# Where the weight sums of the next expert are made: an attention and mixture-of-experts kernel with an order written out by a planner

## The chip, the cores and the metric

The kernel runs on one core of one Trainium2 chip. The metric is the device time of one execution in microseconds (us). Three executions of the kernel before took 963.54, 964.22 and 965.71 us; their median is 964.22 us. The profile shows one further execution, which took 963.27 us.

Engine names are those of the profile: PE is the matrix engine (TensorE), PEld its weight loads, DVE VectorE, ACT ScalarE, POOL GpSimd, SP the engine that only issues DMAs here.

## The reference

```
def phi(x): return np.where(x > 0, x, np.exp(x) - 1.0) + 1.0
# q, k, v: [8 batches, 8 heads, 576 tokens, 64], fp32
q_p, k_p = phi(q), phi(k)
kv  = einsum('bhsd,bhse->bhde', k_p, v);  z = sum(k_p, axis=2)
att = einsum('bhsd,bhde->bhse', q_p, kv) / (einsum('bhsd,bhd->bhs', q_p, z) + 1e-6)
x   = att.transpose(0, 2, 1, 3).reshape(4608, 512)
P = exp(x @ w_gate - max)                     # [4608, 8], w_gate: [512, 8]
for _ in range(8):                            # Sinkhorn: rows, then columns
    P /= P.sum(1) + 1e-9;  P /= P.sum(0) + 1e-9;  P *= 4608 / 8
for e in range(8):                            # w1: [8, 512, 1024], w2: [8, 1024, 512]
    out += P[:, e:e+1] * (maximum(x @ w1[e], 0) @ w2[e])
```

The experts hold nearly all the arithmetic: eight times a 4608 x 512 x 1024 and a 4608 x 1024 x 512 product.

## The kernel before, in words

**Stages.** The attention works on 16 jobs n = 0 to 15 (a batch and half of its heads each). Each loads k, q and v (line 274, from SP's queue except n = 2 to 5, which POOL issues) and leaves its part of the transposed x in SBUF (`xT`, fp16). Expert 0 runs beside it, nine groups g of 512 tokens, as plain matmuls (lines 590 and 859) for the first five groups and in the seven-product form below for layer 1 of the last four. The Sinkhorn loop runs on DVE in the same stretch. Experts 1 to 7 follow, from about 200 us on.

**Seven products in place of eight.** From expert 1 on both layers use a Strassen-Winograd scheme: each matrix is cut into 2 x 2 blocks, and seven block products replace eight, at the price of sums of blocks. The sums of x (four per group) are made once, with the raw blocks written to a scratch tensor in DRAM (`xd`) and read back for every expert (line 665). The sums of w1 are `W` (four DVE additions, line 922, tiles W1, W2, W4, W3 in this order) and of w2 `T` (four DVE subtractions, line 938, T1 to T4, kept in a tile that the profile calls `h`). They are made anew for each expert, from weights that have landed. The sums of the hidden layer are `S` (line 968, four per group). The seven products of layer 1 are m1 to m7 (lines 737 and 742), the adding of a PSUM bank and a kept partial with the relu is line 780 on DVE; the job of that kind which closes product 7 is recorded as "22" (`pe_id[(u, "b22")]`). Layer 2's seven products are line 997. DVE adds most of their banks into the accumulator `acc`, times P (line 1011); the second product's bank goes by ACT (line 1018) and is added by POOL, from SBUF to SBUF (line 1021).

**Units.** A unit is one group of one expert, so nine units (0 to 8) make an expert. In the hand-written order (`order`, line 1085) a unit's own layer-1 products are called a1 to a7 and b1 to b7 (its two pairs of column blocks), A1 to A6 are those of the next unit, and y1 to y7 are layer 2 of the unit two before. PE runs exactly this order:

`y1 y5 y2 a7 y6 y3 a4 b1 b5 y7 b6 b3 b2 b7 A1 A5 y4 b4 A6 A3 A2`

Product y7 adds into the bank that y6 has used, and waits until DVE has taken that bank out.

**The planner.** Everything else is ordered by a list scheduler in the kernel (`_Plan`), which runs when the program is built. Each job names its engines, the jobs it depends on, the buffers it takes and a priority (lower goes first); the scheduler plays the program through with costs of its own and so fixes, for each engine, the order of its instructions. On the chip each engine runs its list strictly in order, and the framework adds semaphore waits for the data and the buffers alone. A dependency that is not one of data, like the gates below, acts on the place in the list and makes no wait on the chip. A table at the end (`ranks`, line 1098) overrides priority, and sometimes the engine, of single jobs by number; it covers the attention, expert 0 and two jobs of expert 1. Jobs 838 to 1045 are those of the last four groups of expert 0.

**Places that the change touches.** The weight loads (line 219, issued from POOL's queue, which also holds POOL's additions) come from expert 2 on in four parts per matrix, into two buffers in turn, so that expert e takes the buffer of e-2; each part is gated by a product 5 of the preceding expert. `W` and `T` have six slots each for four tiles per expert: the first two sums find a free slot early, the third and fourth need the slots of the preceding expert's first and second. The sums carry priority -900 for experts from 2 on, ahead of all else on DVE. In `x_blocks`, `f_st` (line 644) stores the sums of x and `f_raw` (lines 613 and 615, three DMAs per group) the raw blocks, both from SP's queue; `in_prev[0]` is the last q, k or v load that was issued, which is that of job 15 when `x_blocks` runs.

Of the kernel before, what the change touches and what calls it, by code (L numbers as in the profile page):

```python
# [122 lines left out]
def kernel(  # L123
# [20 lines left out]
    NG = N // 512  # L144
# [7 lines left out]
    add = S_.add  # L152
# [87 lines left out]
    w_last, in_prev, w_part = [None], [None], {}  # L240
# [318 lines left out]
    t_close = add(("none", 0.0), f_close, deps=front_ids, prio=0.0)  # L559
# [45 lines left out]
    def x_blocks(g):  # L605
        bs = range(512 * g // S, (512 * g + 511) // S + 1)
        deps = [xt_done[(b, c)] for b in bs for c in range(NDT)]
        t0 = 512 * g
        early = g < NX
        gt_ = S_.grp(p_xse if early else p_xst)  # L610

        def f_raw(_):
            nc.sync.dma_start(out=xd[g // 2][:, g % 2, 0], in_=xT[:, 0:2, t0:t0 + 256])
            for b in range(2):
                nc.sync.dma_start(out=xd[g // 2][:, g % 2, 1 + b], in_=xT[:, 2:4, t0 + 256 * b:t0 + 256 * b + 256])
        last = first = None
        for i in range(3):
            def f_T(_, i=i):
                if i == 0 and early:
                    h_ = (len(p_xse["order"]) - 1) % 2  # L620
                    gt_["tile"] = (acc[NA - 1][:, 2 * h_:2 * h_ + 2, :].bitcast(FP16)
                                   .rearrange("p a (b c t) -> p (a b) c t", b=2, c=2))
                elif i == 0:
                    gt_["tile"] = accp[2].tile([P, 4, 2, 256], FP16, tag="xst", name="xst")
                T = gt_["tile"]
                lo, hi = xT[:, :, t0:t0 + 256], xT[:, :, t0 + 256:t0 + 512]
                if i == 0:
                    nc.vector.tensor_tensor(out=T[:, 0], in0=hi[:, 0:2], in1=lo[:, 0:2], op=ALU.subtract)
                    nc.vector.tensor_tensor(out=T[:, 2], in0=hi[:, 2:4], in1=hi[:, 0:2], op=ALU.subtract)
                elif i == 1:  # L630
                    nc.vector.tensor_tensor(out=T[:, 1], in0=hi[:, 2:4], in1=T[:, 0], op=ALU.subtract)
                else:
                    nc.vector.tensor_tensor(out=T[:, 3], in0=lo[:, 2:4], in1=T[:, 1], op=ALU.subtract)
            last = add(("dve", 0.8 if i == 0 else 0.42), f_T,
                       deps=deps + [v_land[NG + 1 + g] if early else t_close, last] +
                       ([xst_of[g - 1][2]] if i == 0 and g > NG - NL else []),
                       acq=[gt_] if i == 0 else [], use=[gt_], prio=g - 8.0)
            first = first or last
            x_users.append(last)

        xst_of[g] = gt_, last, first

        def f_st(_):
            nc.sync.dma_start(out=xd[g // 2][:, g % 2, 3:7].rearrange("p i c t -> p (i c t)"),
                              in_=gt_["tile"].rearrange("p i c t -> p (i c t)"))
        ti = add(("sp", 0.45), f_st, deps=[last], use=[gt_], prio=0.0)
        out_ = [add(("dma", 1.5), lambda _: None, deps=[ti], use=[gt_], prio=0.0, lat=2.6)]
        ti = add(("sp", 0.9), f_raw, deps=deps + [ti], prio=0.0)
        out_.append(add(("dma", 1.0), lambda _: None, deps=[ti], prio=0.0, lat=2.6))
        x_users.extend(out_)  # L650
        if early:
            xse_done.append(out_[0])
        return out_
# [250 lines left out]
    def combos(e):  # L904
        gw1, tw1, gw2, tw2 = w_t[e]
        gW, tW, gT, tT = {}, {}, {}, {}
        last = wt_prev[0]
        for n, i in enumerate((1, 2, 3, 4) if e == 0 else (1, 2, 4, 3)):
            gW[i] = S_.grp(p_W)

            def f_W(_, i=i):
# [8 lines left out]
                else:  # L920
                    a0, a1, op = w[:, 2:4, 0:512], gW[2]["tile"], ALU.subtract
                nc.vector.tensor_tensor(out=gW[i]["tile"], in0=a0, in1=a1, op=op)
            last = tW[i] = add(("dve", 0.685), f_W, deps=tw1 + [t_close, last, pe_id.get((NG * (e - 1) + min(n, 1) + 5, "b22"))],
                               acq=[gW[i]], use=[gw1] + ([gW[i // 2]] if i in (2, 4) else []),
                               prio=-900.0 if e > 1 else 4.5)
        wt_prev[0], last = last, wt_prev[1]
        for i in range(1, 5) if e > 0 else ():
            gT[i] = S_.grp(p_T)

            def f_T(_, i=i):  # L930
# [5 lines left out]
                          (w[:, 4:8, 256:512], w[:, 0:4, 256:512]),  # L936
                          (w[:, 4:8, 0:256], gT[2]["tile"])][i - 1]
                nc.vector.tensor_tensor(out=gT[i]["tile"], in0=a0, in1=a1, op=ALU.subtract)
            last = tT[i] = add(("dve", 0.685), f_T, deps=tw2 + (h0_users if e == 1 else []) + [x_closed[0], last, pe_id.get((NG * (e - 1) + (i + 15) // 2, ("a22", "b22")[(i + 15) % 2]))],
                               acq=[gT[i]], use=[gw2] + ([gT[i // 2]] if i in (2, 4) else []),  # L940
                               prio=-900.0 if e > 1 else 5.0)
        wt_prev[1] = last
# [130 lines left out]
    x_closed[0] = add(("none", 0.0), f_xclose, deps=x_users, prio=0.0)  # L1073
    for e in range(1, E):
        if e >= 2:
            wg = [[pe_id[(NG * (e - 1) + u + v, f"{n}5")] for v in (0, 2) for n in "ab"] for u in (0, 4)]
            w_t[e] = (load_w1(e, prio=float(e), parts=4, gates=wg[0], deps=w_t[e - 1][1][1:]) +
                      load_w2(e, prio=float(e), parts=4, gates=wg[1], deps=w_t[e - 1][3][1:]))
        co = combos(e)
        for g in range(NG):  # L1080
            if e == E - 1 and g == NG - 1:
                unit_plain(e, g, *co[0:2])
            else:
                unit(e, g, *co)
# [10 lines left out]
    for d, k_ in zip(chain, chain[1:]):  # L1095
# [85 lines left out]
        809:-98.0027 810:-49.9991 811:-50.0237 812:-50.0231 813:-50.0006 814:-50.0132 815:-50.0009 816:-50.0093  # L1181
        817:-49.9718 818:-49.9847 819:-50.0192 820:-49.9832 821:-49.976 822:-49.9994 823:-50.0009 824:8.7515
        825:-98.0234 826:-50.0075 827:-50.0078 828:8.7506 829:8.7428 830:8.7509 831:8.7491:act 832:-49.9745:act
        833:8.7572 834:8.7455 835:-50.0054 836:-49.9853:act 837:-50.0162:dve 838:-49.9829 839:-49.9826 840:-98.0237
        841:-50.0114 842:-50.0075 843:-98.0243 844:-49.9841 845:-50.0201 847:-49.9742 850:-98.0255 851:-49.976
        852:-50.0132 853:-50.024 854:-49.9976 855:8.7518 856:-50.021 857:-50.0078 858:-49.9745 859:-49.9844
        860:-50.0225 861:-98.0156 862:-50.0198 863:-49.9997 864:-50.0087 865:-50 866:-49.976 867:-98.0231 868:-50.0027
        869:8.7542 870:-50.0057 871:8.7443 872:-98.0222 873:-50.0216 874:-50.0177 875:-98.0015 876:-50.0159
        877:-50.0201 878:-50.021 879:8.7443 880:8.4603 881:-50.006 882:8.4591 883:-50.0195 884:8.4594 885:-98.0243
        886:-50.0258 887:-50.0174:act 888:-98.0216 889:-50.0009:act 890:-49.9991 891:-49.9991:dve 892:-98.0036:act  # L1190
        893:-50.018 894:-49.9829 895:-49.982 896:-97.9988 897:8.7434 899:8.744 902:-98.0225 903:-50.018 904:-50.0186
        905:8.7431 906:8.4666 907:-98.0249 908:-50.0237 909:-98.0231 910:-49.9823 911:-98.0231 912:-50.0177
        913:-49.9739 914:8.4609 915:-50.0069 916:8.4672 917:-49.9754 918:8.4672 919:-98.0264 920:-50.0249 921:-49.9988
        922:-50.0231 923:8.7347 924:-50.0186 925:-98.0234 926:-49.9733 927:-50.0234 928:-50.0018 929:-97.9991
        930:8.7368 931:-50.0063 932:-50.0036 933:15.4873 934:8.4711 935:15.4924 936:8.4543 937:-50.0186
        938:-97.9892:dve 939:-50:act 940:-50.0069:dve 941:-50.0237 942:8.7497:act 943:-50.0225:act 944:-49.9907
        945:-49.9997:dve 946:-50.0231 947:-98.0039 948:-50.0009 949:-50.0021 951:-50.0069 954:-49.9739 955:-50.0159
        956:-50.0066 957:8.7422 958:-49.9727 959:-97.9997 960:8.4681 961:8.7521 962:-50.0153 963:-98.0252 964:-50.003
        965:-49.9895 966:8.4729 967:-50.0267 968:8.472 969:8.7506 970:-50.003 971:-50.0018 972:8.4726 973:-98.0261
        974:8.4741 975:-50.0027 976:8.7362 977:-50.021 978:-50.0156 979:-50.0222 980:-50.0021 981:-50.0204 982:15.5131  # L1200
        983:-50.0114 984:-50.0021 985:15.5068 986:8.7497 987:15.5047 988:-50.0255 989:15.4978 990:-50.0009
        991:8.7575:act 992:-50.0222 993:-50.0234 994:-49.9895:dve 995:8.7395:act 996:-50.0162:act 997:-49.9757
        998:-50.0081 999:8.7452 1000:8.7473 1001:-50.024 1003:-50.0069 1006:15.4879 1007:-50.0015 1008:15.4912
        1009:-50.0129 1010:-50.0015 1011:-50.0102 1012:-49.979 1013:-98.0243 1014:-50.015 1015:-50.0252 1016:15.4912
        1017:-50.0018 1018:-50.0039 1019:-50.0159 1020:-50.0063 1021:-50.0186 1022:-50.0003 1023:-50.0234 1024:15.4918
        1025:8.7578 1026:15.4846 1027:-50.0003 1028:-98.0255 1029:-50.0234 1030:-50.0135 1031:-50.0171 1032:-49.988
        1033:-50.015 1034:15.5164 1035:15.5173 1036:15.5077 1037:15.5077 1038:8.756 1039:15.5089 1040:-50.0198
        1041:15.5035 1042:-50.0105:act 1043:-50.0105:dve 1044:-50.0246:act 1045:-98.0045:act 1129:-390.9916
        1144:-390.9907
    """  # L1210
    for w in ranks.split():
        n, p, *en = w.split(":")
# [35 lines left out]
```

## Time and profile before

| what | value |
|---|---|
| median of three executions | 964.22 us (963.54 to 965.71) |
| the profiled execution | 963.27 us |
| its span, first to last instruction | 961.4 us |
| PE busy | 952.0 us, 99% of the span |
| DVE, ACT, POOL busy | 771.1, 570.1, 153.1 us |
| granted PE clock | 0.999 of full speed |
| DMA, mean over the span | 127 GB/s |

The difference between the execution's time and its span, 1.9 us, lies ahead of the first and behind the last instruction. PE's busy time is the union of the modelled stretches of its matmuls. A matmul's duration there includes its passage through the array (273 ns for 256 columns), while in a run of them one starts every 109 ns; an idle gap shorter than the difference does not show as idle. The time from one start to the next is therefore what tells whether PE lost time.

### The profile page before, as it was taken

Reading aid. Unit: us, or ns where it says so; the run is one execution under the profiler, and the core shown is the slowest. Engines: PE = TensorE matmul, PEld = TensorE weight load, DVE = VectorE, ACT = ScalarE, POOL = GpSimd, SP = SyncE. Lnnn points to the kernel's source line nnn. Section 1 sums busy time; section 2 is a strip of 40 time slices with the busy share of each in tenths; the row PEclk is TensorE's granted clock in tenths of the full one; section 3 lists DMA queues with packets and bytes.
Section 4 is the critical chain, followed back from the end, with each engine's and each line's share of the span. In section 5 each row is a group of like instructions: output and inputs, shape, how many; then the busy total and the mean of one; then the engine's idle time right before and its main releaser. Section 6 shows DMA issues by size and latency. Waiting matters only on the chain.

```text
span 961.4 us, 18780 instructions
## 1 busy us (share of the span) xinstructions
PE 952.0 (99%) x7265; PEld 650.3 (68%) x7265; DVE 771.1 (80%) x1530; ACT 570.1 (59%) x1031; POOL 153.1 (16%) x199
## 2 busy tenths in 40 slices
PE   9999999999999999999999999999999999999998
PEld 4666666566676667766676666766677666766676
DVE  6898888977887777987877778977778778877776
ACT  6897755865555555555555555555555555555552
POOL 4100000001111111121112111121112111111111
PEclk9999999999999999999999999999999999999999
DMA  9987982234344432444334432533324433425545
GB/s 318 340 318 262 270 238 82 33 89 100 77 137 108 99 81 65 106 99 100 77 98 96 99 93 67 143 96 94 78 69 100 99 99 78 137 78 150 156 106 132
DMA packets 109946, 121.83 MB, mean 127 GB/s; under 512 B 7840, under 2 KB 92960, under 8 KB 109856
## 3 DMA queue, kind: packets, MB, share of 16 engines
q1 hardware_dynamic: 84320, 96.23, 31.9%
q0 software_dynamic: 25136, 23.87, 14.8%
q8 instruction: 57, 0.93, 0.4%
q10 hardware_dynamic: 400, 0.52, 0.2%
q14 instruction: 33, 0.27, 0.1%
HBM read 119.69 MB, written 17.69 MB: 143 GB/s over the span
## 4 chain that ended last, share of the span: by engine, by line
PE 89%; DVE 5%; DMA 2%; ACT 2%; issue 1%; POOL 0%; DVEq 0%
PE ye L997 32%; PE hq L737 20%; PE att L737 10%; PE ye L859 6%; PE Zye L997 5%; PE Zye L737 5%; PE hq L742 3%; PE hq L590 2%; PE att L742 1%; DVE S L968 1%; DMA kqin<-in_k_dram 1%; DMA kqin<-in_q_dram 1%; DVE acc L1011 1%; DVE h L780 1%; PE xt_ps L418 1%
## 5 line engine op out<-in xcount | busy, mean ns | idle before, releaser
L1011 DVE SCALAR_TENSOR_TENSOR acc<-ye,P_sb,acc 128x256 f32<-128x256 f32 x620 | 266.4, 476 | 106.0 <-PE ye L997 104.2
L997 PEld LDWEIGHTS <-S 128*128 128x128 f16 x1984 | 194.0, 98 | 49.4 <-issue 3.8
L1021 POOL TENSOR_TENSOR acc<-acc,h 128x256 f32<-128x256 f32 x124 | 102.7, 844 | 602.4 <-ACT h L1018 602.4
L997 PE MATMUL ye<-h,S 128*128 128x256 f16 x1488 | 192.8, 273 | 2.6 <-DVE acc L1011 2.6
L997 PEld LDWEIGHTS <-h 128*128 128x128 f16 x1488 | 145.6, 98 | 39.9
L777 ACT ACTIVATE h<-hq 128x512 f16<-128x512 f32 x134 | 80.1, 598 | 142.4 <-PE hq L737 123.4
L737 PEld LDWEIGHTS <-W 128*128 128x128 f16 x896 | 87.6, 98 | 81.4
L737 PE MATMUL hq<-xs,W 128*128 128x512 f16 x448 | 133.3, 379 | 0.0
L737 PE MATMUL att<-xs,W 128*128 128x512 f16 x448 | 133.3, 379 | 0.0
L737 PE MATMUL hq<-xs,w 128*128 128x512 f16 x448 | 124.1, 379 | 0.0
L780 DVE CUSTOM_DVE_ANT_0 h<-att,s 128x512 f16<-128x512 f32 x126 | 86.3, 685 | 26.4 <-ACT s L764 26.4
L737 PEld LDWEIGHTS <-w 128*128 128x128 f16 x672 | 65.7, 98 | 54.8
L774 ACT ACTIVATE h<-Zye 128x512 f16<-128x512 f32 x134 | 80.1, 598 | 33.9 <-PE Zye L737 27.0
L1018 ACT ACTIVATE h<-Zye,P_sb 128x256 f32<-128x256 f32 x124 | 52.1, 471 | 78.4 <-PE Zye L997 78.4
L764 ACT COPY s<-hq 128x512 f32<-128x512 f32 x126 | 73.5, 583 | 38.3 <-PE hq L737 30.7
L780 DVE CUSTOM_DVE_ANT_0 h<-hq,s 128x512 f16<-128x512 f32 x126 | 86.3, 685 | 9.0 <-PE hq L737 9.0
L757 ACT COPY Zye<-hq 128x512 f32<-128x512 f32 x134 | 77.9, 582 | 24.4 <-PE hq L737 17.3
L968 DVE TENSOR_TENSOR S<-h 128x1024 f16<-128x1024 f16 x124 | 85.0, 686 | 5.9 <-ACT h L777 5.9
L771 ACT COPY s<-att 128x512 f32<-128x512 f32 x126 | 74.6, 592 | 0.0
L859 PE MATMUL ye<-w,h 128*128 128x512 f16 x296 | 73.5, 379 | 0.0
L737 PE MATMUL Zye<-xs,w 128*128 128x512 f16 x224 | 66.6, 379 | 0.0
L997 PE MATMUL ye<-w,S 128*128 128x256 f16 x496 | 64.3, 273 | 0.0
(119 smaller groups left out, 1100.3 us busy)
## 6 DMA issues: line engine op xcount, KB each, us to landing
xs<-xd SPq DMA_DIRECT2D x196, 256.0 KB, 4.1
w<-in_moe_w_dram POOLq DMA_DIRECT2D x48, 256.0 KB, 4.1
out_dram<-acc SPq DMA_DIRECT2D x67, 128.0 KB, 2.4
kqin<-in_k_dram SPq DMA_DIRECT2D x12, 576.0 KB, 5.0
kqin<-in_q_dram SPq DMA_DIRECT2D x12, 576.0 KB, 6.6
vin<-in_v_dram SPq DMA_DIRECT2D x12, 576.0 KB, 7.2
xs<-xd SPq DMA_DIRECT2D x49, 128.0 KB, 2.7
xd<-xT SPq DMA_DIRECT2D x27, 128.0 KB, 5.2
```

Source lines behind the costliest of these rows:

```text
L737: nc.tensor.matmul(dst, lhsT=lhs(0, c), rhs=X(b)(c), start=(first and c == 0), stop=(c == 1), skip_group_check=True)
L757: nc.scalar.copy(out=Zt[1], in_=gX["tile"])
L764: nc.scalar.copy(out=gs2["tile"], in_=gX["tile"])
L771: nc.scalar.copy(out=gs5["tile"], in_=gR["tile"])
L774: nc.scalar.activation(out=hd(0, 0), in_=Zt[1], func=AF.Relu)
L777: nc.scalar.activation(out=hd(1, 0), in_=gX["tile"], func=AF.Relu)
L780: nc.vector._custom_dve(TENSOR_ADD_SAT, out=dst, in0=ps, in1=sb, s0=3.0e38, s1=0.0)
L859: nc.tensor.matmul(gy[tt]["tile"], lhsT=hx(f, P * tt, P), rhs=gw2["tile"][:, f, :], start=(f == 0), stop=(f == NFT - 1))
L968: nc.vector.tensor_tensor(out=gS[i]["tile"], in0=a0, in1=a1, op=op)
L997: nc.tensor.matmul(bank(g_)[:, s, :], lhsT=lhs(s, kk), rhs=rhs(kk), start=(new and s == 0 and kk == 0), stop=(kk == 3), skip_group_check=True)
L1011: nc.vector.scalar_tensor_tensor(out=dst(), in0=bank(g_)[:, s, :], scalar=P_sb[:, gg, e:e + 1], in1=dst(), op0=ALU.mult, op1=ALU.add)
L1021: nc.gpsimd.tensor_tensor(out=dst(), in0=dst(), in1=gst["tile"], op=ALU.add)
```

## The change

Three edits of dependencies, one of gates, and new entries in `ranks`:

- `f_W`: the first sum of w1 for expert e may be placed from unit 3 of the preceding expert on (before: unit 5), the others from unit 4 on (before: unit 6).
- `f_T`: sums 1 to 4 of w2 may be placed after the closing job "b22" of units 5, 6, 7 and 8 of the preceding expert. Before they were placed after a22 and b22 of unit 8 and a22 and b22 of unit 0 of the expert itself.
- The gates of the parts of w1 were products 5 of pairs 0a, 0b, 2a and 2b, those of w2 4a, 4b, 6a and 6b; now they are 0a, 0b, 1a, 2a and 2b, 3a, 4a, 4b.
- `f_raw` may only be placed behind the last q, k or v load.
- 56 entries of `ranks` get other values: 44 for PE jobs of the last four groups of expert 0, ten for DVE and ACT jobs there (of which three also get or lose a fixed engine), and two for DVE jobs of unit 0 of expert 1.

No instruction is added or removed.

```diff
@@ x_blocks
-        ti = add(("sp", 0.9), f_raw, deps=deps + [ti], prio=0.0)
+        ti = add(("sp", 0.9), f_raw, deps=deps + [ti, in_prev[0]], prio=0.0)
@@ combos
-            last = tW[i] = add(("dve", 0.685), f_W, deps=tw1 + [t_close, last, pe_id.get((NG * (e - 1) + min(n, 1) + 5, "b22"))],
+            last = tW[i] = add(("dve", 0.685), f_W, deps=tw1 + [t_close, last, pe_id.get((NG * (e - 1) + min(n, 1) + 3, "b22"))],
...
-            last = tT[i] = add(("dve", 0.685), f_T, deps=tw2 + (h0_users if e == 1 else []) + [x_closed[0], last, pe_id.get((NG * (e - 1) + (i + 15) // 2, ("a22", "b22")[(i + 15) % 2]))],
+            last = tT[i] = add(("dve", 0.685), f_T, deps=tw2 + (h0_users if e == 1 else []) + [x_closed[0], last, pe_id.get((NG * (e - 1) + i + 4, "b22"))],
@@ the loop over experts
-            wg = [[pe_id[(NG * (e - 1) + u + v, f"{n}5")] for v in (0, 2) for n in "ab"] for u in (0, 4)]
+            wg = [[pe_id[(NG * (e - 1) + int(x[0]), x[1] + "5")] for x in w.split()] for w in ("0a 0b 1a 2a", "2b 3a 4a 4b")]
@@ ranks (job:priority[:engine]); a few of the 56
-        879:8.7443 880:8.4603 882:8.4591 884:8.4594 906:8.4666 916:8.4672
+        879:-50.0126 880:-50.0249 882:-50.0183 884:-97.9976 906:-50.0063 916:-98.0036
-        933:15.4873 934:8.4711 935:15.4924 982:15.5131 985:15.5068 1034:15.5164 1035:15.5173 1041:15.5035
+        933:-98.0231 934:11.585 935:11.5853 982:11.585 985:11.5886 1034:11.5973 1035:-49.9841 1041:-49.9778
-        938:-97.9892:dve 943:-50.0225:act 997:-49.9757 1045:-98.0045:act 1129:-390.9916 1144:-390.9907
+        938:-50.027 943:-390.9841:act 997:-390.9853:act 1045:8.7398 1129:-390.0186 1144:-390.0144
```

## The prediction

> **What bounds the kernel now.** I read the page's busy times first, then the list of waits, then the chain around one place that the waits named, then the timelines of PE, DVE and POOL there, and last the sums by unit. The page and the waits:
>
> ```profile
> PE 952.0 (99%) x7265; PEld 650.3 (68%) x7265; DVE 771.1 (80%) x1530; ACT 570.1 (59%) x1031; POOL 153.1 (16%) x199
> ...
> PE ye L997 <- DVE acc L1011: 2.6, 6, 0.4
> ```
>
> PE is the bound, so a gain can only come out of time in which PE starts nothing. The second line is the only repeated wait of PE: layer 2 waited six times for an eviction on DVE. The six lie 110.07 us apart (280.25, 390.31, 500.38, ...), one at each change of expert from 1 to 2 up to 6 to 7. The chain and the timelines of PE and POOL at the first:
>
> ```profile
> 277.70 0.50 issue
> 278.20 1.21 DVE h L938
> 279.41 0.80 DVE acc L1011 x2
> 280.20 0.04 issue
> 280.25 1.03 PE ye L997 x8
> ...
> 279.22 0.60 PE L742 MATMUL att<-xs,W 128*128 128x256 f16 x4
> 280.25 1.03 PE L997 MATMUL ye<-h,S 128*128 128x256 f16 x8 [0.43 <-DVE acc L1011]
> ...
> 277.00 1.86 POOL L1021 TENSOR_TENSOR acc<-acc,h 128x256 f32<-128x256 f32 x2 [10.76 <-ACT h L1018]
> ```
>
> The columns are start, duration and what. T1, the first sum of the next expert's w2, stands on DVE ahead of the two evictions of y6, and y7 can't start before they are out. Four products begin at 279.22 at 0.109 us each (eight take 0.87), so y7 was due at 279.66 and came at 280.25: 0.59 us are lost, of which 0.43 shows as idle. T1 also runs long:
>
> ```profile
> L938 DVE TENSOR_TENSOR h<-w x14: 679/692/1216, 197.9 to 850.8; 128x1024 f16<-128x1024 f16 x14
> L922 DVE TENSOR_TENSOR W<-w x16: 637/678/682, 129.4 to 832.2; 128x1024 f16<-128x1024 f16 x16
> ```
>
> Minimum, median and maximum in ns: the same kind of sum takes 692 in the median and 1216 at these six places, where it begins 0.52 us into POOL's second addition (277.68 to 278.86). The units of expert 2, from unit 3 to 6, 8 and the one behind it:
>
> ```profile
> 322.96:335.12 12.16, 12.16 (x87) 8.21 (x85) 7.54 (x16) 6.94 (x13) 2.10 (x3) 1.00 0.50 130
> 335.12:347.28 12.16, 12.16 (x87) 8.23 (x85) 11.01 (x23) 6.94 (x13) 2.54 (x3) 1.00 0.30 67
> 347.28:359.44 12.16, 12.16 (x86) 8.23 (x85) 8.13 (x17) 6.94 (x13) 2.10 (x3) 1.00 0.47 121
> 359.44:371.59 12.15, 12.15 (x86) 8.20 (x85) 11.52 (x24) 6.94 (x13) 2.54 (x3) 1.00 0.19 32
> ...
> 383.74:396.05 12.31, 11.88 (x102) 9.75 (x100) 12.28 (x24) 6.61 (x13) 2.34 (x3) 1.00 0.43 128
> 396.05:408.20 12.15, 12.15 (x86) 8.20 (x85) 10.43 (x21) 6.93 (x14) 2.44 (x4) 1.00 0.50 92
> ```
>
> Behind the length come the busy times of PE, PEld, DVE, ACT and POOL. PE is full everywhere but in the boundary unit, where DVE's 12.28 us exceed a unit's 12.15.
>
> **The change, part by part.**
>
> *T1 and T2 leave the boundary.* T1 holds DVE from 278.20 to the next start at 279.33, 1.13 us; T2 (284.68 to 285.28) 0.60. Without T1 the evictions of y6, done by PE at about 277.6, follow the sum S at 278.20 and end 0.87 us later, at 279.07 (their x2 rows take 0.87). That is 0.59 ahead of y7's due time of 279.66, so the whole 0.59 goes, not a part. What is late next: W4 and W3 stay, since their slots are those of W1 and W2 of the old expert, read last by b5 (279.22 to 279.66) and b6 (behind y7). W4 then runs from about 279.85 to 280.5, y7's own evictions follow at 280.6, and y4 that needs them comes seven products later. DVE in this unit falls to 12.28 - 1.13 - 0.60 = 10.55 us, below the 11.52 that a unit without loss carries. T3 and T4 keep their places (300.44, 302.61), because they wait for the slots that y5 and y6 of the old expert's unit 8 read. Six boundaries give 6 x 0.59 = 3.5 us. Ends: 2.6 (the idle that shows) and 3.6.
>
> *The four sums in the middle.* T1 and T2 take the places behind b22 of units 5 and 6 that W1 and W2 hold now, with the same 0.68 us, so these two units stay at 8.13 and 11.52. W1 and W2 go to units 3 and 4, of the same parity in the two-unit pattern: 7.54 + 0.68 = 8.2 and 11.01 + 0.60 = 11.6 of 12.16. The cover is DVE's idle time there: behind W1's present place DVE idles 0.45 us before its next eviction (356.62 to 357.30, next 357.75), and in unit 4 0.42 (345.59). Cost 0. If the cover were gone, each sum would cost up to the 0.59 of the row above; below nothing it can't be, since PE is full in these units.
>
> The places matter because of POOL. POOL adds at 350.58 to 351.99 and from 362.74, so the sum at 356.62 is alone, and units 3 and 4 repeat this 24.3 us earlier. At the boundary the sum S at 277.58 remains, 0.1 us ahead of POOL's second addition; one S, at 669.2, began behind it, took 957 ns against a median of 681, and PE lost nothing there.
>
> The Trainium skill has the rule for this in "SBUF — State Buffer", section "Who interferes with whom": a DVE instruction with two SBUF inputs and a GpSimd instruction that reads SBUF exclude each other, and the one that starts first blocks the other for its whole length. The trace agrees with 1216 ns against 692 where POOL began first. The rule speaks against the change in one respect: with S blocked in full at each boundary, T1's 0.52 us of blocking would be S's, the evictions would end near 279.6, and the 3.5 would hold with under 0.1 us to spare; by the rows, with S ahead of POOL, it holds with 0.59.
>
> *The weight parts.* Eight issues per expert of 0.74 to 0.78 us on POOL stay eight. Gates make no wait on the chip, only a place in POOL's list, so today's issues at 285.50, 291.16, 303.84, 315.91, 327.63, 340.23, 351.94 and 364.54 should become, by my estimate from the places of the new gates among POOL's additions, 285.5, 291.2, 291.9, 303.8, 315.9, 316.7, 327.6 and 340.2. The first waits 6.65 us for the old buffer as it does now. None stands long before a POOL addition: the next after 291.9 is at 301.95. w2's buffer is read last by y3 of the old unit 8 at 302.4 to 303.3, before 315.9. A part lands in about 4.1 us: w1 is whole near 308, first needed near 332; w2 near 344.4, needed at 356.6. What shares the DMA engines are the x blocks on SP's queue. The tightest is the fifth block of each pair of units: one issued at 304.3 lands at 308.6 and is used at 310.2, 1.6 us later, with a part issued at 303.84 beside it. That overlap stays for two of the pairs and goes for the third (351.94). Cost 0; ends: 0, and one x block late by the 1.3 us that an overlapped landing took more (5.4 against 4.1, at 285.2), which its 1.6 of slack still holds.
>
> *Raw copies behind the last load.* SP's list today:
>
> ```profile
> 75.77 0.34 SPq L644 DMA_DIRECT2D xd<-acc  x1
> 76.15 0.44 SPq L613 DMA_DIRECT2D xd<-xT  x1
> 76.63 1.37 SPq L615 DMA_DIRECT2D xd<-xT  x2
> 78.10 0.43 SPq L644 DMA_DIRECT2D xd<-acc  x1
> 78.58 0.45 SPq L613 DMA_DIRECT2D xd<-xT  x1
> 79.07 1.61 SPq L615 DMA_DIRECT2D xd<-xT  x2
> 80.78 0.44 SPq L274 DMA_DIRECT2D kqin<-in_k_dram  x1
> ```
>
> The stores of the sums (L644) stay, since they keep their dependencies; the nine copies of groups 0 to 2 go behind the load at 99.73. The loads of job 12 then issue some 3.5 us sooner (77.3), job 14's v 2.4 sooner, job 15's k at least 0.8. The copies then take 5.5 us of SP at about 100.2 to 105.7; behind them stands the store at 103.29, which nothing needs before 128.48. PE has expert 0's work throughout, so earlier data shortens only PE's in-order waits: from 104 to 115 us I find 0.48, 0.23, 0.13 and 0.22 us between starts in excess of the products' own steps, 1.1 in all. I take half, -0.5, because the first of them hangs on job 15's k. Ends: -1.1 and +0.5 (one more wait of the largest size).
>
> *New ranks.* They reorder 44 PE jobs of expert 0 between about 130 and 200 us, where PE is full (69.66 of 70 us) and DVE has 59.66. The same products run, so only waits can change. Between starts I find 0.24 + 0.43 + 0.19 + 0.13 = 1.0 us lost there. Ends: -1.0, and +1.5, three waits of the 0.5 size. I take 0, as neither sign shows in any row.
>
> The sum: -3.5 - 0.5 = -4.0 us against the profiled execution, 963.27 to 959.3. The median stands 0.95 above that execution, which gives 960.2.
>
> **The rivals.** *The boundary stall stays under another name* (W4, W3 or an eviction takes T1's place, or T1 is not moved because its parts land late). For it: DVE still has 24 - 2 jobs there. Against it: 1.6 us of room by the sum above, and 12 us between landing and use. It gives 964.22 - 0.5 = 963.7.
>
> *The sums in the middle push evictions.* For it: units 4 and 6 leave DVE only 0.5 us. Against it: unit 6 holds W2 today and PE lost nothing. If W1 and W2 each cost 0.59 in six experts, 7.1 us come back: 964.2 - 4.0 + 7.1 = 967.3. With this one, the result is slower than before once each of the 24 moved sums costs over 0.25 us.
>
> *Expert 0's new order makes PE wait.* ACT is busy 10.0 of 10 us from 180 to 190 and DVE 9.69 from 170 to 180, so products put earlier can find their banks not yet evicted. At a wait of 0.5 us for one in five of the 44 jobs this costs 4.4 us: 964.6, no change. It takes 5.9 to be slower by more than can be told from no change.
>
> **How the numbers follow.** 0.2% of 964.22 is 1.93 us, about what a measurement of this kernel tells from none: faster means below 962.29. Forecast 0.74 (the ends above, all at once, are 958.5 and 963.6; as a faster result its own range is 958.5 to 962.2); stall under another name 0.09 (963.7, same); middle sums 0.06 (967.3, slower); expert 0's order 0.11, of which 0.03 slower, 0.06 same and 0.02 still faster. So faster 0.76, same 0.15, slower 0.09. The range for 8 in 10 cuts the forecast's far end by little and reaches over the same-size cases: 958.8 to 964.2.
>
> **What would show it.** Right: no wait of PE for DVE in line 997 any more, no L938 row above 0.7 us after 200 us, T1 and T2 where W1 and W2 stand now, 109.5 us from expert to expert in place of 110.07. SP shows L613 and L615 only behind the last L274. Wrong: a PE wait at the old place with W or an eviction ahead; L997 or L737 waiting in units 3 to 6; PE idle over 1 us more between 100 and 200 us; a load in POOL's list that blocks its additions.

## The result, and the profile after

The changed kernel takes 959.84 us (median of six executions, 958.73 to 960.26), the kernel before 964.51 us (six, 963.54 to 965.71). The ratio is 0.9949 with a 95% interval of 0.9937 to 0.9962: 4.7 us faster, and clear of what a measurement tells from no change. The profiled execution took 960.04 us, with a span of 958.3 us against 961.4.

The page's busy times and the longest entries of the waits of PE after the change:

```profile
span 958.3 us, 18782 instructions
...
PE 950.7 (99%) x7265; PEld 650.3 (68%) x7265; DVE 768.7 (80%) x1529; ACT 571.7 (60%) x1032; POOL 153.4 (16%) x199
...
PE yw L510 <- DVE warm L498: 1.3, 1, 1.3
PE num_ps L402 <- DVE xn L407: 1.2, 1, 1.2
PE xt_ps L418 <- ACT P_sb L441: 0.3, 1, 0.3
```

No wait of line 997 for DVE is left. The first remaining one belongs to the warm-up products at the start; the second is new and comes back below. The same boundary as before, in the timelines of PE, DVE and POOL:

```profile
277.03 1.04 PE L997 MATMUL ye<-h,S 128*128 128x256 f16 x8
277.90 1.04 PE L997 MATMUL ye<-w,S 128*128 128x256 f16 x8
278.77 1.04 PE L742 MATMUL hq<-xs,w 128*128 128x256 f16 x8
279.65 0.60 PE L742 MATMUL att<-xs,W 128*128 128x256 f16 x4
280.08 1.04 PE L997 MATMUL ye<-h,S 128*128 128x256 f16 x8
...
278.11 0.68 DVE L968 TENSOR_TENSOR S<-h 128x1024 f16<-128x1024 f16 x1
278.71 1.65 DVE L1011 SCALAR_TENSOR_TENSOR acc<-ye,P_sb,acc 128x256 f32<-128x256 f32 x4
...
277.43 1.95 POOL L1021 TENSOR_TENSOR acc<-acc,h 128x256 f32<-128x256 f32 x2 [10.77 <-ACT h L1018]
```

The evictions of y6 (the first two of the four on DVE at 278.71) now follow the sum S at once and are out by about 279.58, half a microsecond before y7's turn at 280.08. PE goes from product to product without a gap: 279.65 plus four steps of 0.109 is 280.09. The sums of the weights no longer run long (minimum, median and maximum in ns), and the units have no hole. The second fence has the boundary unit of the kernel before (unit 8 of expert 2), and the third units 3 to 6, 8 and the next of the changed kernel. Each row of the two goes from one y1 to the next:

```profile
L938 DVE TENSOR_TENSOR h<-w x14: 679/683/693, 198.4 to 847.7; 128x1024 f16<-128x1024 f16 x14
```

```profile
383.61:396.40 12.79, 12.37 (x105) 9.98 (x103) 12.76 (x25) 6.94 (x13) 2.64 (x3) 1.00 0.43 129
```

```profile
322.64:334.80 12.16, 12.16 (x85) 8.22 (x84) 8.12 (x16) 6.94 (x13) 2.10 (x3) 1.00 0.47 125
334.80:346.96 12.16, 12.16 (x86) 8.22 (x85) 11.53 (x23) 6.94 (x13) 2.55 (x3) 1.00 0.30 73
346.96:359.11 12.15, 12.15 (x85) 8.22 (x84) 8.11 (x16) 6.94 (x13) 1.41 (x2) 1.00 0.31 99
359.11:371.27 12.16, 12.16 (x85) 8.22 (x84) 11.53 (x23) 6.94 (x13) 1.87 (x2) 1.00 0.03 10
...
383.45:395.65 12.20, 12.20 (x104) 9.97 (x102) 12.11 (x24) 6.94 (x13) 2.65 (x3) 1.00 0.44 139
395.65:407.81 12.16, 12.16 (x85) 8.23 (x84) 9.17 (x18) 6.94 (x13) 2.89 (x4) 1.00 0.65 105
```

PE is busy all of every unit, the one at the boundary (383.45) too, which takes 12.20 us where it took 12.79. DVE is still nearly full there, 12.11 of 12.20 us, and PE loses nothing by it.

To say where PE lost time I take, over all its products, the time from one start to the next less the step that products of that shape show when nothing holds them (216 ns for 512 columns, 109 ns for 256, and so on). By this the profile of before lost 3.5 us at the six boundaries, and that of after nothing. But the spans differ by 3.1 only, since the changed kernel's profile lost more between 60 and 120 us: 2.99 against 2.36 us. In that stretch of many short products I count only excesses over 0.1 us, against each shape's median step; with other steps the totals move by 1 us and more, but the difference stays between 0.3 and 0.7. (The expectations below count with slightly other steps, which gives some 0.2 us less.) That part differs between profiles of the same program, as the experiments show, and the profiled execution of the kernel before was one of its faster ones (963.27 against a median of 964.5).

### The profile page after: what moved, and what is told of

It is laid out like the page before. It is cut to its first block, busy times and chain, and to the rows that moved or that the text cites. A ratio compares the mean times of both kernels' runs of the same rounds, so it can differ in the third digit from the quotient of the medians.

```text
span 958.3 us, 18782 instructions
## 1 busy us (share of the span) xinstructions
PE 950.7 (99%) x7265; PEld 650.3 (68%) x7265; DVE 768.7 (80%) x1529; ACT 571.7 (60%) x1032; POOL 153.4 (16%) x199
## 4 chain that ended last, share of the span: by engine, by line
PE 95%; DMA 2%; ACT 1%; DVE 1%; issue 0%; POOL 0%; SPq 0%; DVEq 0%; ACTq 0%
PE ye L997 34%; PE hq L737 20%; PE att L737 10%; PE ye L859 7%; PE Zye L997 6%; PE Zye L737 5%; PE hq L742 4%; PE hq L590 2%; DMA kqin<-in_k_dram 2%; PE att L742 2%; PE Zye L742 1%; PE xt_ps L418 1%; PE kv_ps L335 1%; PE num_ps L402 1%; PE qt_ps L363 1%; ACT e L290 1%
## 5 line engine op out<-in xcount | busy, mean ns | idle before, releaser
L997 PE MATMUL Zye<-w,h 128*128 128x256 f16 x496 | 64.3, 273 | 0.0
```

What stands on the lines that cost most here:

```text
L997: nc.tensor.matmul(bank(g_)[:, s, :], lhsT=lhs(s, kk), rhs=rhs(kk), start=(new and s == 0 and kk == 0), stop=(kk == 3), skip_group_check=True)
```

## The experiments

Every comparison is with the kernel before on the same chip.

### The sums and the weight parts alone

```diff
-  ... min(n, 1) + 5, "b22" ...        (f_W)
+  ... min(n, 1) + 3, "b22" ...
-  ... (i + 15) // 2, ("a22", "b22")[(i + 15) % 2] ...   (f_T)
+  ... i + 4, "b22" ...
-  gates 0a 0b 2a 2b | 4a 4b 6a 6b
+  gates 0a 0b 1a 2a | 2b 3a 4a 4b
```

> Only the three edits of the sums and weight parts; raw copies and ranks as before. My theory (the gain is the boundary stall): 3.5 us faster than before, near 961.0; the six waits of PE line 997 for DVE are gone, the time from expert to expert goes from 110.07 to 109.5 us, the stalls of 104 to 115 us stay at about 1.1 us. Rival (the gain comes from the front, raw copies and new ranks): no change, 964.5, and 4.7 us in the other two edits.

Measured: 960.25 us against 964.31, ratio 0.9955 (0.9942 to 0.9969). The six waits are gone. A second comparison on the same chip as the whole change (below) gave 961.10 against 964.79, ratio 0.9962 (0.9949 to 0.9975). So 3.7 to 4.1 us, where the boundaries account for 3.54; both intervals hold that figure. Most of the gain is that of the sums, not of the front. One expectation was missed: the stalls of 104 to 115 us, which were to stay at 1.1 us, were 0.7 here (and 0.4 with the ranks alone), with the same instructions in the same order up to that time.

### Which sum, and whether it is DVE's load

Two kernels move only T with w2's gates, or only W with w1's.

```diff
   e5:  f_T as after the change; f_W as before; gates 0a 0b 2a 2b | 2b 3a 4a 4b
   e6:  f_W as after the change; f_T as before; gates 0a 0b 1a 2a | 4a 4b 6a 6b
```

> Of the three edits only that of T and the gates of w2's parts; W1 and W2 stay in units 5 and 6. My theory (T1 alone makes the stall, through POOL): the full 3.5 us of the boundaries, near 961, no wait of PE for DVE left; T1, T2 then share units 5 and 6 or the next ones with W1, W2 without a loss of PE. Rival (all four sums together overload the boundary): part of the stall stays, 962 to 963.

> Of the three edits only that of W and the gates of w1's parts; T1 and T2 stay at the boundary. My theory: nothing, 964.3, six waits of 0.43 us stay, T1 1.21 us. Rival (the load of DVE as a whole): part of the stall goes, 962 to 963.

Moving T alone: 961.87 us against 964.24, ratio 0.9981 (0.9967 to 0.9995), and no wait of line 997 left. By the starts of products the boundaries lose nothing, but behind unit 6 of each preceding expert 0.10 us are lost, since W2 and T2 now stand one behind the other there. So T alone gains 2.9 us in the trace, not the 3.5 expected. The measured gain is 2.4, with an interval of 0.5 to 3.2 us.

Moving W alone: 964.65 against 964.24, ratio 1.0004 (0.9995 to 1.0013), nothing. Its waits of PE and its row of T1:

```profile
PE ye L997 <- DVE acc L1011: 2.6, 6, 0.4
...
L938 DVE TENSOR_TENSOR h<-w x14: 683/692/1211, 198.1 to 850.9; 128x1024 f16<-128x1024 f16 x14
```

All six waits are as before, with T1 as long as before. The stall is T's. What W2's move gains is that T2 doesn't have to share its place.

### T1 left where it was, POOL moved away

This kernel tells the place of T1 in DVE's list from the collision with POOL. Only the place of two additions per boundary in POOL's list is changed: they go behind the weight load that waits for its buffer. PE, DVE, ACT and SP run the same instructions in the same order as in the kernel before.

```diff
-    fin_prev[(gg, dh)] = add(("pool", 0.8), f_g, ...)
+    fin_prev[(gg, dh)] = add(("pool", 0.8), f_g, ...); late.setdefault((e, g), []).append(fin_prev[(gg, dh)])
...
-    co = combos(e)
+    co = combos(e); [S_.dep(k_, w_t[e][1][0] - 1) for k_ in late.get((e - 2, 6), ())]
```

> The kernel before, T1 and T2 left at the boundary; only POOL's two additions of group 6 are listed behind the first weight part of the expert after next, so that POOL adds some 9 us later (about 286 in place of 277) at the boundaries 1 to 2 up to 5 to 6; the boundary 6 to 7 has no such part and keeps the collision. My theory (T1's blocking by POOL is 0.52 of the 0.59): at five boundaries T1 takes 0.69 us, y7 comes at most 0.1 us late, 2.5 us faster, near 962.0; at the sixth T1 still takes 1.21 and PE waits 0.43. Rival (T1's mere place ahead of the evictions is enough): all six waits stay, 964.5.

Measured: 961.55 us against 964.31, ratio 0.9970 (0.9958 to 0.9981), 2.8 us faster. The first boundary in its timelines of PE, DVE and POOL:

```profile
279.62 0.60 PE L742 MATMUL att<-xs,W 128*128 128x256 f16 x4
280.10 1.03 PE L997 MATMUL ye<-h,S 128*128 128x256 f16 x8
...
277.98 0.68 DVE L968 TENSOR_TENSOR S<-h 128x1024 f16<-128x1024 f16 x1
278.58 0.68 DVE L938 TENSOR_TENSOR h<-w 128x1024 f16<-128x1024 f16 x1
279.18 1.26 DVE L1011 SCALAR_TENSOR_TENSOR acc<-ye,P_sb,acc 128x256 f32<-128x256 f32 x3
...
285.36 0.78 POOL L219 DMA_DIRECT2D w<-in_moe_w_dram  x1 [18.73 <-PE hq L742]
286.16 2.38 POOL L1021 TENSOR_TENSOR acc<-acc,h 128x256 f32<-128x256 f32 x2
```

T1 is still ahead of the evictions, but POOL adds only at 286.16, and T1 takes 0.68 us. y7 was due at 279.62 + 0.44 = 280.06 and comes at 280.10: 0.05 us late, and so at five boundaries. The sixth, which had no weight load to hide behind, is the control within the same run (PE and DVE):

```profile
827.25 0.60 PE L742 MATMUL att<-xs,W 128*128 128x256 f16 x4
828.27 1.03 PE L997 MATMUL ye<-h,S 128*128 128x256 f16 x8 [0.42 <-DVE acc L1011]
...
826.22 1.21 DVE L938 TENSOR_TENSOR h<-w 128x1024 f16<-128x1024 f16 x1
```

There the collision stays, with 1.21 us of T1 and the same 0.59 us lost. So the blocking makes all but 0.05 of the 0.59; T1's place in front of the evictions alone would almost not have mattered. The rule of the Trainium skill ("SBUF — State Buffer", section "Who interferes with whom"), that of two such instructions the second waits for the first to end, is what both boundaries show, to about 0.1 us: at the sixth T1 began with 0.66 us of POOL's addition left and took 0.53 longer. Five times 0.54 is 2.7 us, and 2.8 were measured.

T1 is the last of a chain of three. POOL's second addition began 0.10 us behind a sum S on DVE, and took 1.17 us against a median of 0.72. So S held POOL up first, and it is the lengthened addition that T1 then ran into.

### Each moved sum made twice

```diff
-    nc.vector.tensor_tensor(out=gW[i]["tile"], ...)
+    for _ in range(2 if e > 1 and i < 3 else 1): nc.vector.tensor_tensor(out=gW[i]["tile"], ...)
     (and the same for gT)
```

> The changed kernel, with each of the four moved sums made twice, one behind the other, for experts 2 to 7 (24 sums of 0.68 us more on DVE, the order otherwise the same). My theory (units 3 to 6 have the room; 0.42 to 0.57 us idle behind each sum, and another such amount before PE waits): the time stays within 0.5 us of the changed kernel, 959.5 to 960.3, no PE wait. Rival (DVE in units 4 and 6 is nearly full and the evictions behind it are what PE waits for): 0.2 to 0.6 us for each sum of units 4 and 6, 2.4 to 7 us more, 962 to 967.

Measured: 962.74 us against 964.24, ratio 0.9981 (0.9973 to 0.9990); 2.9 us above the changed kernel's 959.84, and 2.7 above the kernel with the sums and the raw copies (960.05, below), which was measured beside it. Here the rival is right at its lower end. Unit 6 of expert 1, DVE and PE:

```profile
259.85 1.41 DVE L938 TENSOR_TENSOR h<-w,h 128x1024 f16<-128x1024 f16 x2
261.18 0.87 DVE L1011 SCALAR_TENSOR_TENSOR acc<-ye,P_sb,acc 128x256 f32<-128x256 f32 x2
...
261.45 0.59 PE L737 MATMUL Zye<-xs,w 128*128 128x512 f16 x2
262.11 1.03 PE L997 MATMUL ye<-w,h 128*128 128x256 f16 x8
```

and the same place in the changed kernel:

```profile
259.76 0.68 DVE L938 TENSOR_TENSOR h<-w,h 128x1024 f16<-128x1024 f16 x1
260.36 0.87 DVE L1011 SCALAR_TENSOR_TENSOR acc<-ye,P_sb,acc 128x256 f32<-128x256 f32 x2
...
261.36 0.59 PE L737 MATMUL Zye<-xs,w 128*128 128x512 f16 x2
261.79 1.04 PE L997 MATMUL ye<-w,h 128*128 128x256 f16 x8
```

y1 of the next unit takes the bank that y4 has left, so it waits for the two evictions behind the sum. In the changed kernel these are out at 261.23 and y1 begins at 261.79, 0.56 us later. In the doubled one y1 begins 0.06 us after they are out (262.05 and 262.11), so the room was 0.5 us. The second sum moves the evictions by 0.73 us against the products, and y1 comes 0.23 us late (262.11 after 261.45 + 0.43). Twelve even units times 0.23 are 2.7 us of the 2.9; in the odd units 3 and 5 nothing is lost. The 0.10 of the kernel that moves T alone is the same margin: a second sum 0.60 behind the first, less 0.5.

### The raw copies and the ranks

```diff
   e2:  f_raw: deps=deps + [ti]  ->  deps=deps + [ti, in_prev[0]]
   e3:  the 56 new ranks
   e9:  both
   e7:  the raw copies with the sums and weight parts, ranks as before
```

> Only the raw copies behind the last load. My theory: the loads of jobs 12, 14 and 15 issue 0.8 to 3.5 us sooner, the PE stalls from 104 to 115 us fall from 1.1 to 0.5 us or less, the time by 0.5 to 1.1 us to about 963.7; the six boundary waits of 0.43 us stay. Rival (the copies were hidden, the stalls there come from the order on DVE): the stalls stay at 1.1 us, 964.5.

> Only the 56 new ranks. My theory: the same products in another order, time the same within 0.5 us, 964.5; PE's lost time from 120 to 200 us stays near 1.0 us and that from 104 to 115 near 1.1. Rival (the ranks give the part of the gain that the boundaries don't): 963.4, 1.1 us faster.

> The three edits and the raw copies, ranks as before. If the copies are worth what they gave alone (0.7 us): 959.6, 0.7 below the edits alone (960.25) and the same as the whole change. Rival (PE's lost time of the front only moves from one place to another, 60 to 120 us together 2.1 to 2.8 in all profiles so far): 960.3, no different from the edits alone; the lost time of 60 to 120 us stays at 2.1 to 2.8.

> The raw copies and the new ranks together, sums and weight parts as before. If the two pieces are worth what they gave alone (0.7 and 0.4 us): 963.1, 1.1 us faster than before. If PE's lost time of the front only moves: 964.2, with 60 to 120 us again at 2.1 to 2.9 us. The six boundary waits of 0.43 us stay in both.

> The changed kernel, beside the next one on the same chip. If the front is worth 1.1 us: 1.1 below the edits of the sums alone. If it only moves lost time: within 0.5 us of them.

> The edits of the sums and weight parts alone once more, for the comparison with the whole change: 3.5 to 4.1 us below the kernel before; the whole change 1.1 us lower still, or within 0.5 us of it.

| kernel | us | before | ratio (95%) |
|---|---|---|---|
| raw copies alone | 963.59 | 964.31 | 0.9987 (0.9978 to 0.9996) |
| ranks alone | 963.88 | 964.31 | 0.9995 (0.9986 to 1.0003) |
| both | 963.11 | 964.79 | 0.9985 (0.9976 to 0.9994) |
| sums and weight parts | 960.25, again 961.10 | 964.31, 964.79 | 0.9955, 0.9962 |
| sums, weight parts, raw copies | 960.05 | 964.24 | 0.9952 (0.9940 to 0.9965) |
| the whole change again | 960.26 | 964.79 | 0.9953 (0.9941 to 0.9966) |

The raw copies make the kernel faster by a little, alone and with the ranks: both intervals stay below 1. On top of the sums the comparisons give 0.2 us (960.25 to 960.05) and for raw copies and ranks 0.4 and 0.8 (960.25 to 959.84, 961.10 to 960.26), none of it outside the scatter. Only the last pair was measured side by side, five executions each, and its 0.8 lies between the two forecasts, 1.1 and under 0.5; so does the 0.2 against 0.7 and nothing. Whether the front's gain adds to that of the sums stays open. The ranks alone are not told from nothing.

The trace of SP after the change begins its part as the prediction said, but not in all of it:

```profile
77.19 1.30 SPq L644 DMA_DIRECT2D xd<-acc  x2
78.64 0.38 SPq L274 DMA_DIRECT2D kqin<-in_k_dram  x1
...
94.69 0.34 SPq L644 DMA_DIRECT2D xd<-acc  x1
97.46 0.37 SPq L274 DMA_DIRECT2D vin<-in_v_dram  x1
...
99.31 0.42 SPq L274 DMA_DIRECT2D vin<-in_v_dram  x1
99.79 0.52 SPq L613 DMA_DIRECT2D xd<-xT  x1
```

Over the seven profiles without the moved copies and the six with them: job 12's k issues at 80.8 to 82.0 us without and 78.2 to 78.6 with; job 14's v at 96.0 to 98.1 and 97.0 to 97.5, no sooner, as SP waits there (2.3 us in the trace of after) for ACT's cast of an earlier v, line 234; the last load, job 15's v, lands at 107.8 to 109.1 and 107.1 to 108.4, 0.8 us sooner in the mean. PE's lost time between 104 and 116 us is 0.24 to 1.72 us without and 0.12 to 0.26 with. But between 60 and 80 us it is 0.24 to 1.48 without and 1.29 to 1.80 with, so that 60 to 120 us together hold 2.4 to 3.3 and 2.5 to 3.0. The first product of layer 2 of expert 1 starts at 200.58 to 201.84 (mean 201.06) and 200.49 to 201.01 (mean 200.76). The means differ by 0.3 us, within the spread of so few profiles; the long cases are missing with the move.

The stall at 71 us, the new wait in the list of after (product 402 for the eviction at line 407), follows a late load. DVE, in the order of its list, waits for job 11's k, and the eviction stands behind:

```profile
71.09 0.76 DVE L303 TENSOR_SCALAR t<-kqin 128x1152 f16<-128x1152 f32 x1 [1.41 <-DMA kqin<-in_k_dram]
71.76 0.68 DVE L407 TENSOR_TENSOR xn<-num_ps,rden 128x512 f16<-128x512 f32 x1
72.50 0.28 PE L402 MATMUL num_ps<-kvz,qpT 128*128 128x128 f16 x2 [1.16 <-DVE xn L407]
```

That load, issued at 64.4 to 65.0 us in all thirteen profiles, lands at 69.2 and 69.3 in the two without the stall and at 70.0 to 71.1 in the others. SP's list up to that load is the same in all of them. It was late in all six with the moved copies and in five of the seven others, which is no difference that so few profiles can show. Why its landing varies is open.

## Why the prediction was right, point by point

**Total and chances.** 960.2 us was forecast and 959.84 measured; the gain was put at 4.0 us and is 4.7 by the medians of six. The 3.5 for the boundaries is shown by the single kernels. The 0.5 for the front lies within their scatter and is not shown on top of the sums, so that the total came within 0.4 us is partly luck.

**T1 and T2 leave the boundary, 3.5 us.** Right in mechanism and size: 0.59 us at six places became 0. The room before y7, foreseen as 0.59, is 0.5 (evictions out at about 279.58, y7 at 280.08). W4 came later than foreseen (at 280.88, where 279.85 would be about 280.3 in this trace's time), as another S stands before it, and nothing waited for it. The statement that the lock makes 0.52 of T1's length was borne out by moving POOL away: 0.54 of the 0.59. The unfavourable case, S blocked by POOL in T1's stead, did not come: S began 0.03 to 0.10 us ahead of POOL's second addition at all six boundaries and took 0.68 to 0.69 us.

One reading beside it was wrong: that DVE's load at the boundary would fall to 10.55 us and leave 1.6 of room. From one y1 to the next DVE was busy 12.76 of 12.79 us before, and is 12.11 of 12.20 now, since jobs that stood behind T1 and T2 come sooner. (The row of 12.31 us in the prediction ends 0.35 us ahead of the next y1, so it is no whole unit.) The load of the unit was thus no measure of the stall: what counted was when the two evictions of y6 were out.

**The sums in the middle, 0.** Right for the cost, and for the load: 8.2, 11.6, 8.13 and 11.52 us of DVE were foreseen in units 3 to 6, and 8.12, 11.53, 8.11 and 11.53 came. The cover was named only in part. In unit 5 DVE still idles 0.45 us behind the sum. In unit 4 the 0.42 us were less than the sum's 0.60: it leaves no idle time, and its evictions begin about 0.1 us later against the products than before. What kept PE from waiting there is the 0.5 us between the evictions and y1. The expectation of the doubled sums counted both amounts in all four units; in units 4 and 6 only the second is there. The rival "the sums in the middle push evictions" had the right mechanism for twice the load; with one sum per unit they come about 0.1 us later in the even units, and PE does not wait.

**The weight parts, 0.** Right. POOL's list after the change, from the first load of the second expert on:

```profile
285.35 0.78 POOL L219 DMA_DIRECT2D w<-in_moe_w_dram  x1 [5.97 <-PE hq L742]
289.64 1.41 POOL L1021 TENSOR_TENSOR acc<-acc,h 128x256 f32<-128x256 f32 x2 [3.51 <-ACT h L1018]
291.00 1.53 POOL L219 DMA_DIRECT2D w<-in_moe_w_dram  x2
301.79 1.94 POOL L1021 TENSOR_TENSOR acc<-acc,h 128x256 f32<-128x256 f32 x2 [9.26 <-ACT h L1018]
303.68 0.78 POOL L219 DMA_DIRECT2D w<-in_moe_w_dram  x1
```

The loads stand at 285.35, 291.00, 291.78, 303.68, 315.76, 316.49, 327.47 and 340.07, each within 0.25 us of the estimate. A gate orders the list and holds nothing on the chip.

**Raw copies, -0.5.** The sign holds; the size is 0.2 us on top of the sums (0.4 and 0.8 together with the ranks) and 0.7 alone. Its working holds in part: job 12's loads came some 3 us sooner and the stalls of 104 to 116 us went, as foreseen; job 14's v did not come 2.4 us sooner and job 15's k 0.5 in the mean in place of 0.8, and lost time between 60 and 80 us, which was as high in some profiles without the move, took back most of what went. The term was right through less than it was built from, which is luck.

**Ranks, 0.** Not told from nothing (0.9995, 0.9986 to 1.0003). PE lost 1.0 to 1.1 us from 120 to 200 us with the old ranks and 0.9 to 1.0 with the new (excesses over 0.03 us counted here): 0.1 us.

**The rivals.** The stall did not stay under another name. The order of expert 0 did not make PE wait. Of the middle sums it is said above.

## What to carry to other kernels

When PE is full but for a short wait that comes back once per stage, read its last releaser, and then whether that instruction was longer than its like: here 1216 ns against a median of 692 led to a collision with POOL, and moving T1 took the whole wait away, moving POOL all but 0.05 us of it. Before work is moved into a stage that looks idle, the room that counts is the time from the eviction behind it to the product that needs the bank (0.5 us here), not the engine's idle share; one sum fitted and a second cost 0.23 us. Terms under 1 us in a front that waits for loads need many executions: PE's lost time from 60 to 120 us varied by 1.0 us over seven profiles that run the same order there.

## What the runs showed of the hardware that I had not expected

With both additions moved to 286.16, POOL's pair took 2.38 us against 1.41 to 1.95 elsewhere, while of the two sums S on DVE beside it the one that had begun 0.24 us earlier took 0.83 (0.81 to 0.83 at all five boundaries) and the one that began 0.03 earlier 0.67. Most of the price falls on the one that comes second, but the first was not wholly spared: 0.15 us, against 0.46 on POOL's first addition. Why the S that was 0.24 ahead paid and those 0.03 to 0.10 ahead did not is open. On POOL's side it cost nothing here. The landing of one and the same load at 65 us varied from 69.2 to 71.1 us between executions, which moves the whole front by as much as the smaller pieces of this change.
